# Issuing the copies of the block means from GpSimd's queue in place of SyncE's, in an attention and expert kernel

## The chip, the cores and the metric

The kernel runs on one core of a Trainium2 chip. The metric is the device time of one execution, in microseconds (us). Several executions are timed and the median is taken; one more execution is recorded by the hardware profiler, and all rows shown here come from that one. The engines are TensorE (PE in the rows, with PEld for its weight loads), VectorE (DVE), ScalarE (ACT), GpSimd (POOL) and SyncE (SP). The last two also issue DMAs; SPq and POOLq are their queues of such instructions.

## The reference

The program chains three layers in float32. The change lies in the first one, the attention, which is cut down here to what it computes; the two that follow are a mixture of 8 experts (each of 1536 tokens goes to two of them) and a dense layer with squared ReLU.

```python
def _attn_ref(q, k, v):                       # (2, 8, 768, 64) each
    B, H, S, D = q.shape
    block, window = (32, 16)
    nb = S // block                           # 24 blocks
    k_sum = k.reshape(B, H, nb, block, D).max(axis=3)
    v_sum = v.reshape(B, H, nb, block, D).mean(axis=3)
    scores_l = scale * q @ k^T, kept where |i - j| < window
    scores_s = scale * q @ k_sum^T + log(block)
    a = softmax(concat([scores_l, scores_s]))
    return a @ concat([v, v_sum])

x = moe(attention output)                     # top 2 of 8 experts, w1, relu, w2
return moe2(x)                                # w_in, relu squared, w_out
```

Each query thus sees its near keys and, for every block of 32 positions, one key (the maximum of the block) and one value (the mean of the block).

## The kernel before

**Units and tiles.** The 2 x 8 heads are worked in pairs: a unit u (0 to 7) is a batch and a pair of heads (u = 4 b + hp). For each unit SyncE loads three tiles from DRAM: `kB` (keys of both heads, 2 DMAs of 200 KB), `qt` (queries, 384 KB) and `vB` (values, 576 KB). `vB` holds 12 windows of 96 positions, so that 96 partitions by 12 x 128 elements come from DRAM; partitions 96 to 119 of every window take the 24 block means of the unit. There are LBUF = 4 buffers of each kind, so unit u + 4 takes the buffers of unit u once that one is done with.

**The block means.** `vmean(u)` (line 303) lets TensorE work out the 24 means from the loaded part of `vB`, 12 matmuls into one PSUM tile; `vcopy(u)` (line 317) is VectorE's copy of that to the tile `vm`, of which there are two buffers; `vstore(u)` (line 321) copies `vm` into the last 24 partitions of `vB`, the same 6 rows into all 12 windows, by four DMAs of 36 KB each. For unit 0 two engine copies (`vput`, lines 311 and 313) do this instead, so seven units have a `vstore`, 28 DMAs in all.

**The rest of the attention.** A step s is a unit and one or two tiles of 128 queries. `scores` (line 336, TensorE), `least` (line 347, VectorE: mask and row minimum), `expo` (line 354, ScalarE), `trans` (line 362, TensorE), `e_copy` (line 366, ScalarE), `pv` (line 377, TensorE: needs the whole of `vB`, the means included) and `x_cols` (lines 385 and 387). Then, by tiles g of 128 tokens (0 to 11; 6 of each batch), `rows` (line 397) and `x_row` (line 401) turn the result into rows; `gate_cols`, `gate_copy`, `gate_turn` and `gate_rows` (lines 432 to 451) compute the gates; `route` (lines 455 to 578; its matmuls are lines 500 to 511, its slots lines 518 and 522) finds each token's slot at its two experts; `scatter` (line 421) lets GpSimd write the rows to their slots in the DRAM buffer `xg` by indirect DMAs, two of them per tile. When the 18 scatters of tiles 0 to 8 have landed, SyncE loads the first expert's tokens (`x_load(0)`, line 213); tiles 9 to 11 reach that expert by one-hot matmuls (line 470). With that done, the experts' matmuls begin (lines 748 to 750), and they fill TensorE to the end of the program.

**What sets the order.** All of the attention is put in order by `Plan`, a list scheduler that runs while the kernel is written out. A `node` has an engine letter (P TensorE, V VectorE, A ScalarE, G GpSimd, D SyncE's queue), a cost in us, the nodes it depends on, and a `wait` that is added to its end for those who depend on it (for a load, LW = 0.9). The scheduler picks the node that can start first, with the longest remaining chain ahead among these, and writes out its instructions; each engine then runs its instructions in that fixed order. So a node's engine, cost and wait move the instructions of other engines too. A buffer is free for its next user when the nodes named by `plan.free` are over: the reload of `vB` for unit u + 4 is released by the last `pv` of unit u.

```python
    def load(cost, fn, *deps, **kw):
        return node("D", cost, fn, *deps, wait=LW, **kw)
    ...
    pn = node("P", 0.33 * n, lambda s=s: pv(s), cn, *vst[u], take=("v",))
    ...
    plan.free(v0, "w", vm, *pv_u[u])
```

SyncE's queue runs in order, and its loads are chained (`seq`, `after`) as kB, qt, vB of unit 0, then of unit 1, and so on. A DMA on SyncE's queue also waits until the one eight places ahead of it on that queue has landed.

Of the kernel before, what the change touches and what calls it, by code (L numbers as in the profile page):

```python
# [28 lines left out]
NQB = S // QB  # L29
WK = QB + 2 * WIN  # L30
# [19 lines left out]
LBUF = 4  # L50
# [25 lines left out]
class Plan:  # L76
# [6 lines left out]
    def node(self, eng, cost, fn, *deps, take=(), wait=0.0, after=()):  # L83
        n = {"id": len(self.nodes), "eng": eng, "cost": cost, "fn": fn, "deps": deps, "after": after, "take": take,
             "wait": wait, "free": {}}
        self.nodes.append(n)
        return n
# [48 lines left out]
def moe_pipeline_kernel(ctx: ExitStack, tc: tile.TileContext, qT, kT, vW, mk, idm, wg, noise, w1, w2, out):  # L136
    nc = tc.nc
# [97 lines left out]
    def attention(ctx):  # L235
# [15 lines left out]
        vB = [ac.tile([128, NQB, 128], F32, name=f"vB{i}") for i in range(LBUF)]  # L251
# [18 lines left out]
        node = plan.node  # L270
# [22 lines left out]
        p_t, e_t, et_t, xrow, z_t = {}, {}, {}, {}, {}  # L293
# [13 lines left out]
        def vput(a, eng):  # L307
            h = NQB // 2
            o, i = vB[0][WK:NS, a * h:a * h + h, :], p_t["m", 0][WK:NS, None, 0:128].to_broadcast([NB, h, 128])
            if a:  # L310
                nc.scalar.activation(out=o, in_=i, func=AF.Copy)
            else:
                v.tensor_copy(out=o, in_=i)

        def vcopy(u):
            p_t["c", u] = wk.tile([128, 128], F32, name="vm", bufs=2)
            v.tensor_copy(out=p_t["c", u], in_=p_t["m", u][:, 0:128])

        def vstore(u):
            for c in range(4):  # L320
                nc.sync.dma_start(out=vB[u % LBUF][WK + 6 * c:WK + 6 * c + 6],
                                  in_=p_t["c", u][32 * c:32 * c + 6, None, :].to_broadcast([6, NQB, 128]))

        def cols(b, hp, t):
            return xT[b][hp][:, t * 128:(t + 1) * 128]
# [263 lines left out]
        def load(cost, fn, *deps, **kw):  # L589
            return node("D", cost, fn, *deps, wait=LW, **kw)  # L590

        km, sc, ld_v, vst, qn, prev = {}, {}, {}, {}, {}, []
# [3 lines left out]
        for u in range(len(heads)):  # L596
# [25 lines left out]
            vm = node("P", 0.75 if u else 2.6, lambda u=u: vmean(u), ld_v[u], id_n, take=("v",))  # L622
            if u:
                vc = node("V", 0.2, lambda u=u: vcopy(u), vm, take=("vm",))
                vst[u] = [load(0.41, lambda u=u: vstore(u), vc)]
                plan.free(vm, "v", vc)
                plan.free(vc, "vm", *vst[u])
            else:
                vst[u] = [node("V", 0.85, lambda: vput(0, None), vm), node("A", 0.7, lambda: vput(1, None), vm)]
                plan.free(vm, "v", *vst[u])  # L630
            if u == 1:
# [3 lines left out]
                    out=xg[0:CAP, :].rearrange("r d -> (r d)").rearrange("(p a c) -> p a c", p=128, a=4),  # L635
                    in_=zt[:, None, :].to_broadcast([128, 4, CAP])), set_n, after=[wvals_n])
# [5 lines left out]
        for s, (b, hp, t0, n) in enumerate(order):  # L642
            u = b * HP + hp
# [92 lines left out]
    with ExitStack() as actx:  # L736
        attention(actx)
# [634 lines left out]
```

## Time and profile before

| | us |
|---|---|
| median of 3 runs (lowest, highest) | 696.1 (695.59, 696.43) |
| the profiled execution: its time | 692.52 |
| the profiled execution: its span | 690.5 |
| TensorE busy over the span | 640.0 (93%) |
| VectorE busy | 440.9 (64%) |
| ScalarE busy | 365.7 (53%) |
| GpSimd busy | 100.0 (14%) |

The span is the time from the first instruction to the last in the profile, and the time of that execution is 2.0 us more. The profiled execution is 3.6 us shorter than the median of the runs. Issuing a DMA is not counted as busy time on SyncE. In a row of a timeline stand the start in us from the span's start, the length in us, the engine, the line of the kernel, the operation, the tile that it writes and those that it reads, and the number of instructions merged into the row; in square brackets the idle time of the engine ahead of it, and what ended that. Most of TensorE's float32 matmuls stand twice in the trace: 8 instructions of `pv` are 16 records.

### The profile page before, as it was taken

The numbers are of one execution on the slowest core, as the hardware profiler recorded it, in microseconds if no ns is written. First come the engines' busy times: TensorE is split into PE (matmuls) and PEld (weight loads), VectorE is DVE, ScalarE is ACT, GpSimd is POOL, SyncE is SP. The second block draws the span as 40 slices with busy tenths as digits, with TensorE's granted clock in tenths as the row PEclk, the third lists the DMA queues.
The fourth block names the chain that finished last, engine by engine and source line by source line (L and its number), as shares of the span: only waits on it lengthen the run. The fifth ranks groups of instructions, "written<-read, shape, count | busy, mean of one in ns | idle before, by whom it ended". The sixth has DMA issues, their size and how long they took to land. (4 is left out here: it accounts for less than half of the span.)

```text
span 690.5 us, 11121 instructions
## 1 busy us (share of the span) xinstructions
PE 640.0 (93%) x3928; PEld 572.5 (83%) x3928; DVE 440.9 (64%) x980; ACT 365.7 (53%) x708; POOL 100.0 (14%) x171
## 2 busy tenths in 40 slices
PE   5697866799999999999999999999999999999995
PEld 4576646698999999999999998888878888788884
DVE  5567744686778887767777867666554566554442
ACT  3594551256566656666667666655443544433431
POOL 3000244420101000610004000310042100200002
PEclk9999977799999999999999999999999999999998
DMA  8969435478999998889889898665446544342201
GB/s 205 198 165 211 130 123 166 160 255 288 311 322 289 332 260 292 211 272 265 257 222 391 246 309 244 241 185 159 144 127 207 158 150 122 108 136 91 93 1 64
DMA packets 75740, 139.98 MB, mean 203 GB/s; under 512 B 9041, under 2 KB 44161, under 8 KB 74894
## 3 DMA queue, kind: packets, MB, share of 16 engines
q1 hardware_dynamic: 69566, 116.95, 58.0%
q0 software_dynamic: 6112, 22.25, 8.6%
q8 instruction: 33, 0.54, 0.3%
q14 instruction: 29, 0.24, 0.1%
HBM read 103.27 MB, written 34.88 MB: 200 GB/s over the span
## 5 line engine op out<-in xcount | busy, mean ns | idle before, releaser
L748 PE MATMUL ph<-xh,wh 128*128 128x512 f32 (+8 forms) x448 | 162.8, 363 | 1.8 <-ACT xh L1188 1.8
L750 PE MATMUL ph<-xl,wh 128*128 128x512 f32 (+8 forms) x448 | 162.7, 363 | 1.5 <-DVE xl L1189 1.2
L749 PE MATMUL ph<-xh,wl 128*128 128x512 f32 (+8 forms) x448 | 162.4, 363 | 0.0
L192 DVE TENSOR_TENSOR wl<-wr,wh 128x1024 fp32r<-128x1024 f32 x112 | 136.8, 1221 | 35.2 <-ACT wh L188 32.2
L188 ACT ACTIVATE wh<-wr 128x1024 fp32r<-128x1024 f32 x112 | 117.6, 1050 | 10.3 <-DMA wr<-in_w_dram 7.1
L750 PEld LDWEIGHTS ph<-xl,wh 128*128 128x128 f32 x448 | 84.2, 188 | 10.4 <-DVE xl L1189 2.1
L748 PEld LDWEIGHTS ph<-xh,wh 128*128 128x128 f32 x448 | 84.3, 188 | 10.1 <-ACT xh L1188 2.6
L749 PEld LDWEIGHTS ph<-xh,wl 128*128 128x128 f32 x448 | 84.3, 188 | 7.4
L750 PE MATMUL acc<-hl,wh 128*128 128x416 f32 (+7 forms) x256 | 87.8, 343 | 1.3 <-DVE hl L772 1.3
L749 PE MATMUL acc<-hh,wl 128*128 128x416 f32 (+7 forms) x256 | 87.7, 342 | 0.0
L748 PE MATMUL acc<-hh,wh 128*128 128x416 f32 (+7 forms) x256 | 87.7, 342 | 0.0
L765 ACT ACTIVATE hr<-ph 128x512 f32<-128x512 f32 x48 | 28.7, 598 | 100.3 <-PE ph L750 97.8
L766 DVE SCALAR_TENSOR_TENSOR hg<-ph,hr 128x512 f32<-128x512 f32 x48 | 33.2, 692 | 70.1 <-ACT hr L765 68.2
L749 PE MATMUL acc<-wh,hl 128*128 128x512 f32 x192 | 74.8, 390 | 0.0
L750 PE MATMUL acc<-wl,hh 128*128 128x512 f32 x192 | 74.7, 389 | 0.0
L748 PE MATMUL acc<-wh,hh 128*128 128x512 f32 x192 | 74.7, 389 | 0.0
L771 ACT ACTIVATE hh<-ph 128x416 fp32r<-128x416 f32 (+7 forms) x64 | 32.1, 502 | 80.2 <-PE ph L750 74.8
L772 DVE SCALAR_TENSOR_TENSOR hl<-ph,hh 128x416 fp32r<-128x416 f32 (+7 forms) x64 | 36.5, 570 | 34.5 <-ACT hh L771 32.0
L769 DVE TENSOR_TENSOR hl<-hg,hh 128x512 fp32r<-128x512 f32 x48 | 33.3, 694 | 33.5 <-ACT hh L768 32.8
L768 ACT ACTIVATE hh<-hg 128x512 fp32r<-128x512 f32 x48 | 30.3, 632 | 38.9 <-DVE hg L766 38.0
L354 ACT ACTIVATE es<-z,bi 128x120 f32<-128x120 f32 x96 | 36.6, 383 | 25.9 <-DVE bi L347 25.9
L750 PEld LDWEIGHTS acc<-hl,wh 128*128 128x128 f32 x256 | 48.2, 188 | 1.8 <-DVE hl L772 1.7
(246 smaller groups left out, 915.5 us busy)
## 6 DMA issues: line engine op xcount, KB each, us to landing
wr<-in_w_dram SPq DMA_DIRECT2D x64, 512.0 KB
wr<-w2f SPq DMA_DIRECT2D x48, 512.0 KB
cr<-in_w_dram SPq DMA_DIRECT2D x32, 512.0 KB
w2f<-c SPq DMA_DIRECT2D x32, 256.0 KB
vB<-in_vW_dram SPq DMA_DIRECT2D x8, 576.0 KB
xin<-xg SPq DMA_DIRECT2D x20, 208.0 KB
kB<-in_kT_dram SPq DMA_DIRECT2D x16, 200.0 KB
yg<-ys SPq DMA_DIRECT2D x16, 192.0 KB
```

The source lines that it names most:

```text
L188: nc.scalar.activation(out=hi_t[i], in_=raw_t[i], func=AF.Copy)
L192: nc.vector.tensor_tensor(out=lo_t[i], in0=raw_t.pop(i), in1=hi_t[i].bitcast(F32), op=OP.subtract)
L354: nc.scalar.activation(out=e_t[s][:, i, h], in_=z, func=AF.Exp, bias=bi, scale=-1.0, accum_out=sums[:, b * QT + t0 + i, c:c + 1])
L748: nc.tensor.matmul(out=o, lhsT=wh, rhs=xh, start=first, stop=False)
L749: nc.tensor.matmul(out=o, lhsT=wl, rhs=xh, start=False, stop=False)
L750: nc.tensor.matmul(out=o, lhsT=wh, rhs=xl, start=False, stop=last)
L765: nc.scalar.activation(out=r[:, 0:n], in_=p[:, 0:n], func=AF.Relu)
L766: nc.vector.scalar_tensor_tensor(out=gg[:, 0:n], in0=p[:, 0:n], scalar=0.0, in1=r[:, 0:n], op0=OP.max, op1=OP.mult)
L768: nc.scalar.activation(out=hh[:, 0:n], in_=gg[:, 0:n], func=AF.Copy)
L769: nc.vector.tensor_tensor(out=hl[:, 0:n], in0=gg[:, 0:n], in1=hh[:, 0:n].bitcast(F32), op=OP.subtract)
L771: nc.scalar.activation(out=hh[:, 0:n], in_=p[:, 0:n], func=AF.Relu)
L772: nc.vector.scalar_tensor_tensor(out=hl[:, 0:n], in0=p[:, 0:n], scalar=0.0, in1=hh[:, 0:n].bitcast(F32), op0=OP.max, op1=OP.subtract)
```

## The change

The four DMAs of `vstore` are issued on GpSimd's queue, and in the plan the node moves from SyncE's queue (cost 0.41, wait 0.9) to GpSimd (cost 2.5, wait 2.0).

```diff
         def vstore(u):
             for c in range(4):
-                nc.sync.dma_start(out=vB[u % LBUF][WK + 6 * c:WK + 6 * c + 6],
-                                  in_=p_t["c", u][32 * c:32 * c + 6, None, :].to_broadcast([6, NQB, 128]))
+                nc.gpsimd.dma_start(out=vB[u % LBUF][WK + 6 * c:WK + 6 * c + 6],
+                                    in_=p_t["c", u][32 * c:32 * c + 6, None, :].to_broadcast([6, NQB, 128]))
 
         def cols(b, hp, t):
             return xT[b][hp][:, t * 128:(t + 1) * 128]
@@ -622,7 +622,7 @@
             vm = node("P", 0.75 if u else 2.6, lambda u=u: vmean(u), ld_v[u], id_n, take=("v",))
             if u:
                 vc = node("V", 0.2, lambda u=u: vcopy(u), vm, take=("vm",))
-                vst[u] = [load(0.41, lambda u=u: vstore(u), vc)]
+                vst[u] = [node("G", 2.5, lambda u=u: vstore(u), vc, wait=2.0)]
                 plan.free(vm, "v", vc)
                 plan.free(vc, "vm", *vst[u])
```

The two lines move instructions on every engine of the attention. Three places follow. In the names, `vB0_112` is the buffer of `vB` for units 0 and 4, `vB1_113` for 1 and 5, `vB2_114` for 2 and 6, `vB3_115` for 3 and 7; `kB_116` to `kB_119` are the same for the keys; `L303` is `vmean`, `L377` is `pv`.

SyncE's queue, from the load of unit 7's values on, as a piece of the difference (minus: before, plus: the change):

```order
 L603 DMA qt<-in_qT_dram 128x768
 L606 DMA vB_115<-in_vW_dram 96x1536
-L321 DMA vB_112<-vm 6x12x128 x4
-L321 DMA vB_113<-vm 6x12x128 x4
-L182 DMA wr<-in_w_dram 128x1024
-L321 DMA vB_114<-vm 6x12x128 x4
-L182 DMA wr<-in_w_dram 128x1024
-L321 DMA vB_115<-vm 6x12x128 x4
-L182 DMA wr<-in_w_dram 128x1024
+L182 DMA wr<-in_w_dram 128x1024 x3
 L213 DMA xin<-xg 32x13x128 x4
```

The copies of units 4 to 7 leave the queue behind the last load, and those of units 1 to 3 leave it between the loads of unit 4; on GpSimd all 28 stand ahead of the first scatter.

TensorE, from the first `pv` of unit 3 to the last `pv` of units 1, 2 and 3, before:

```order
L377 MATMUL pv_747<-et_725,vB3_115 64x64 x8
L362 MATMUL pt_764<-idz_78,es_547 120x128 x4
L362 MATMUL pt_771<-idz_78,es_606 120x128 x4
L432 MATMUL pv_780<-xh_128,wg_sb_121 32x384 x2
L432 MATMUL pv_780<-xl_129,wg_sb_121 32x384 x2
L362 MATMUL pt_788<-idz_78,es_652 120x128 x4
L377 MATMUL pv_796<-et_778,vB1_113 64x64 x8
L377 MATMUL pv_807<-et_786,vB2_114 64x64 x8
L377 MATMUL pv_818<-et_805,vB3_115 64x64 x8
```

and the same place in the change:

```order
L377 MATMUL pv_743<-et_722,vB3_115 64x64 x8
L362 MATMUL pt_760<-idz_78,es_550 120x128 x4
L362 MATMUL pt_770<-idz_78,es_606 120x128 x4
L303 MATMUL pv_778<-vB0_112,idz_78 32x128 x12
L362 MATMUL pt_796<-idz_78,es_664 120x128 x4
L432 MATMUL pv_804<-xh_128,wg_sb_121 32x384 x2
L432 MATMUL pv_804<-xl_129,wg_sb_121 32x384 x2
L377 MATMUL pv_815<-et_792,vB1_113 64x64 x8
L377 MATMUL pv_826<-et_794,vB2_114 64x64 x8
L377 MATMUL pv_837<-et_813,vB3_115 64x64 x8
```

`vmean(4)`, which reads the newly loaded `vB0_112`, now stands ahead of the last `pv` of units 1, 2 and 3, which release the reloads of `vB1_113`, `vB2_114` and `vB3_115`.

TensorE around the first matmul of the routing of tiles 0 to 5 (`L500`), before:

```order
L362 MATMUL pt_1234<-idz_78,es_1108 120x128 x2
L377 MATMUL pv_1239<-et_1223,vB3_115 64x64 x8
L377 MATMUL pv_1253<-et_1232,vB3_115 64x64 x4
L377 MATMUL pv_1261<-et_1249,vB2_114 64x64 x4
L500 LDWEIGHTS ones_81
L500 MATMUL pv_1266<-rowb_82,ones_81 128x48
L336 MATMUL ps_1268<-kB2_118,qt_853 64x2x96 x2
```

and in the change, from the last of the count matmuls of that routing (`L511`) on:

```order
L511 MATMUL pv_1240<-mall_85,ones_81 128x8
L336 MATMUL ps_1270<-kB0_116,qt_445 64x2x96 x2
L336 MATMUL ps_1270<-kB0_116,qt_445 64x2x24 x2
L377 MATMUL pv_1281<-et_1221,vB3_115 64x64 x8
L377 MATMUL pv_1302<-et_1238,vB3_115 64x64 x4
L377 MATMUL pv_1311<-et_1249,vB2_114 64x64 x4
```

The `pv` of unit 7 (`vB3_115`) stood ahead of the routing of tiles 0 to 5, and now stands behind all of its matmuls. On GpSimd, the ninth scatter, where it was the eleventh, is the first one of a row (`xrow`) that is made behind the first matmul of the second routing (tiles 6 to 8): four tiles are scattered ahead of it instead of five, and five instead of four from it to the end of tile 8. Between `vmean(6)` and `vmean(7)` TensorE also does 20 matmuls of `pv` of units 4 and 5 more than before, and one group of 4 in `trans` and one `rows` less.

## Rows read from the trace of the kernel before

**Rows 1.** Two stretches: busy us of PE, PEld, DVE, ACT, POOL, then PEclk, DMA share, GB/s.

```profile
0.00:137.00 137.00, 98.83 (x1226) 80.20 (x1227) 80.32 (x374) 63.16 (x251) 32.22 (x65) 0.86 0.64 171
137.00:500.00 363.00, 361.38 (x1918) 345.27 (x1917) 266.63 (x493) 225.79 (x349) 44.09 (x75) 1.00 0.84 261
```

**Rows 2.** The same, two stretches of the attention.

```profile
44.00:62.00 18.00, 12.51 (x234) 9.63 (x234) 10.15 (x34) 9.44 (x35) 0.00 (x0) 0.99 0.98 226
...
82.00:97.00 15.00, 9.14 (x91) 6.34 (x90) 5.42 (x32) 5.63 (x26) 10.75 (x20) 0.84 0.45 176
```

**Rows 3.** Timeline of SyncE's queue, 43 to 76 us.

```profile
43.98 0.35 SPq L606 DMA_DIRECT2D vB<-in_vW_dram  x1
44.38 1.19 SPq L599 DMA_DIRECT2D kB<-in_kT_dram  x2
...
49.40 0.34 SPq L606 DMA_DIRECT2D vB<-in_vW_dram  x1
...
58.43 8.55 SPq L321 DMA_DIRECT2D vB<-vm  x8
...
72.11 3.08 SPq L321 DMA_DIRECT2D vB<-vm  x4
```

**Rows 4.** Timeline of TensorE, 47 to 82 us.

```profile
47.31 0.52 PE L432 MATMUL pv<-xh,wg_sb 128*32 128x384 f32 x2
...
48.09 0.65 PE L362 MATMUL pt<-idz,es 128*120 128x128 f32 x4
48.67 1.62 PE L377 MATMUL pv<-et,vB 120*64 120x64 f32 x48
...
61.41 1.41 PE L303 MATMUL pv<-vB,idz 96*32 96x128 f32 x24 [1.80 <-DMA vB<-in_vW_dram]
...
67.63 0.86 PE L303 MATMUL pv<-vB,idz 96*32 96x128 f32 x24
...
70.28 1.35 PE L377 MATMUL pv<-et,vB 120*64 120x64 f32 x40
...
78.03 1.50 PE L377 MATMUL pv<-et,vB 120*64 120x64 f32 x32 [2.87 <-DMA vB<-vm]
...
81.09 1.10 PE L336 MATMUL ps<-kB,qt 128*64 128x192 f32 x8
```

**Rows 5.** Timeline of VectorE: the maxima of unit 5, a copy to vm, the first slots.

```profile
50.10 2.00 DVE L291 TENSOR_REDUCE kB<-kB 64x24 f32<-64x768 f32 x2 [3.27 <-DMA kB<-in_kT_dram]
...
69.38 0.29 DVE L317 COPY vm<-pv 128x128 f32<-128x128 f32 x1
...
81.20 0.26 DVE L518 TENSOR_TENSOR sl<-pv,mall 128x96 f32<-128x96 f32 x1 [0.63 <-PE pv L511]
```

**Rows 6.** One line's instructions, lengths in ns as shortest/median/longest: vstore, scatter, a later fill.

```profile
L321 SPq DMA_DIRECT2D vB<-vm x28: 720/726/1376, 24.5 to 74.5; - x28
...
L421 POOL DMA_INDIRECT xg<-xrow,slot_i x24: 968/972/1154, 82.1 to 134.3; - x24
...
L857 POOL DMA_INDIRECT xg<-z,tb_gi x7: 937/938/1856, 151.8 to 228.8; - x7
```

**Rows 7.** Timeline of GpSimd: first and last scatter of two bursts.

```profile
82.11 1.15 POOL L421 DMA_INDIRECT xg<-xrow,slot_i  x1 [74.56 <-DVE bi L347]
...
93.77 0.97 POOL L421 DMA_INDIRECT xg<-xrow,slot_i  x1 [0.22 <-issue]
...
104.68 0.97 POOL L421 DMA_INDIRECT xg<-xrow,slot_i  x1 [9.85 <-DVE sl L518]
...
113.61 0.97 POOL L421 DMA_INDIRECT xg<-xrow,slot_i  x1 [0.23 <-issue]
```

**Rows 8.** Timeline of TensorE and VectorE in the second burst.

```profile
110.35 0.29 PE L377 MATMUL pv<-et,vB 120*64 120x64 f32 x3 [1.07 <-issue]
...
114.63 0.42 DVE L385 COPY xh<-pv 128x256 f32<-128x256 f32 x1 [5.63 <-remote]
```

**Rows 9.** VectorE's first use of the first expert's loaded tokens.

```profile
130.89 2.08 DVE L219 STREAM_TRANSPOSE xtt<-xin 128x416 f32<-128x416 f32 x4
```

## The prediction

> **What bounds the kernel now.** I read the stretches first. From 137 us on TensorE is busy without a break (361 of 363 us), while in the first 137 us it works 98.8 [rows 1]. The experts can't start before the attention ends, and nothing behind them waits for SyncE or GpSimd, so what the change is worth is the shift of that point, us for us. The queues come next. SyncE issues the copies of the block means from 24.5 to 75 us [rows 6]; those of units 4 to 7 stand behind all loads, eight of them taking 8.55 us and the last four 3.08 [rows 3]. In this middle part the DMA engines are 98% busy from 44 to 62 us [rows 2], and TensorE waits for a load at 61.41 and for the copies of unit 7 at 78.03, 2.87 us long [rows 4]. From 82 us on GpSimd issues the scatters in bursts of ten and eight [rows 7]; in these TensorE has gaps of 1.1 us that no wait of the profile explains, and VectorE, idle for 5.63 us, goes on at 114.63 [rows 8], just as the last scatter of the burst is issued (113.61 + 0.97 = 114.58). TensorE is busy in 9.1 of the 15 us from 82 to 97 us [rows 2].
>
> **The change, part by part.** SyncE loses 28 DMAs of 0.73 us, GpSimd gets them. The ones of units 1 to 3 end nothing: no row of TensorE waits for them now, and GpSimd is idle between its set-up and 82.11 us [rows 7]; I count them at nothing. If they came late, `pv` of units 1 to 3 would stall, each by what the copy takes longer. The weight loads behind them on SyncE's queue come earlier, but feed the experts, behind the attention: nothing. What counts is the four places where the order moves.
>
> *The values of unit 4.* `vmean(4)` now stands at the place that TensorE reaches at 47.31 us [rows 4]. Its load is issued at 43.98 [rows 3], when the last `pv` of unit 0 is over, and that place has not moved. It lands shortly before the keys of unit 5, which are queued behind it and are used from 50.10 us on [rows 5]: half of these are 200 KB, 0.9 us at 226 GB/s [rows 2], so it lands near 49.2. TensorE stalls by 1.9 us (bounds: nothing, if it lands by 47.31; 2.8, if only at 50.10). Behind the stall, in order, are `vmean(4)` (0.86, as the row at 67.63), a group of `trans` (0.65), the gate matmuls (48.09 - 47.31 = 0.78) and the last `pv` of unit 1 (a third of 1.62) [rows 4]: 49.2 + 0.86 + 0.65 + 0.78 + 0.54 = 52.0. That `pv` releases the next load of values, issued at 49.40 now [rows 3]: 2.6 us later, and the loads of units 6 and 7 stand behind it. What is queued until then (576 + 400 + 384 KB, 6.0 us at 226 GB/s from some 2 us after 43.98) is through at 52, so the DMA engines run dry for about that long. I take 2.0 us for the loads of units 6 and 7, between 0 and 2.6.
>
> *The copies of unit 7.* `vmean(6)` goes from 61.41 to 63.4. From there to `vmean(7)` are 6.2 us now; TensorE gets 20 more `pv` matmuls there (1.35, the row at 70.28) and loses a `trans` group (0.65) [rows 4], so `vmean(7)` starts at 70.3, against 67.63. VectorE's copy starts 1.75 us after it (69.38) and takes 0.29 [rows 5], so GpSimd can begin at 72.3. How long a plain DMA takes GpSimd to issue no row shows. The nearest are its own scatters, 0.97 us with 0.22 between [rows 6, 7]; SyncE's 0.73 for this very copy is the low bound, the longest fill, 1.86, the high one [rows 6]. With 1.19 four end at 77.1 (bounds 75.2 and 80.6). Now the last issue ends at 75.19 and TensorE goes on at 78.03 [rows 3, 4], 2.8 us later; so they land at 79.9 (78.0 to 83.4).
>
> *The routing of tiles 0 to 5 ahead of `pv` of unit 7.* From the end of `vmean(7)` (68.49) to the first slots are 12.7 us now [rows 4, 5]. Out of these fall the wait (2.87), the `pv` of unit 7 and of the last tile of unit 6 (1.50) and the 1.35 done before: 7.0 remain, so slots come at 78.2 instead of 81.20, 3.0 us earlier. `pv` of unit 7 then waits for 79.9, and ends 1.5 us later, at 81.4. The same work is done now at 82.1, when TensorE is through with the group of scores whose row begins at 81.09 [rows 4] and ends at 82.19, its last matmul overlapping the next by some 0.1. So TensorE is 0.7 us ahead. The late loads have eaten most of the 2.87.
>
> *The scatters.* The first burst starts 3.0 us earlier, at 79.1, with eight in place of ten. At their spacing of 1.3 us [rows 7] it ends near 89.4, where it now ends at 94.7. The second holds ten in place of eight, and lasts 2.6 us longer. The load of the first expert's tokens can only follow it, but is used at 130.89 [rows 9], 16.3 us behind the burst's end now; that covers the 2.6. But VectorE and TensorE were held up to the end of this burst [rows 8], so the 2.6 are on the path. The first burst gives back at most 5.3 us; I take 4.0, since 5.9 of the 15 us from 82 to 97 are idle on TensorE [rows 2] and a part of them is VectorE's and ScalarE's chain. Bounds: 0 and 5.3.
>
> **The sum:** 0.7 + 4.0 - 2.6 = 2.1 us earlier. The profiled execution would go from 692.5 to 690.4. The median of the runs stands 3.6 above that execution, so I forecast 696.1 - 2.1 = **694.0**. With every bound at its good end (no late load 2.0, the whole 5.3) it is 5.4 us earlier; at the bad end (load 0.6 later, copies 3.5 later, nothing back) 6.0 us later, 702.
>
> **Rivals.**
>
> *The longer second burst decides (slower).* Place: GpSimd, from 104.7 us on. If the gaps in the first burst are not on the path, because ScalarE's chain would have filled that time, what is left is -0.7 + 2.6 = +1.9: 698.0. It decides as soon as the first burst gives back less than 1.9 us. For it: VectorE resumes exactly at that burst's end [rows 8]. Against it: the first burst shows the same kind of gaps. Chance 0.20.
>
> *GpSimd's issue is held up by VectorE (slower).* The 24 scatters took 0.97 to 1.15 us [rows 6] in a stretch where VectorE is busy 80 of 137 us [rows 1], which speaks against it; one fill of seven took 1.86. If the copies of unit 7 all took that, they would land at 83.4, and `pv` would stall 3.5 us more: -2.1 + 3.5 = +1.4, 697.5. Chance 0.10. The Trainium skill, "SBUF — State Buffer", section "SBUF: two separate sides", says that GpSimd can't write its DMA descriptors while VectorE runs an operation that takes both ports, and advises to issue from SP instead. By that rule this rival is what happens; the scatters' narrow spread does not bear it out here.
>
> *Nothing to tell (no change).* The first burst gives back 2 us instead of 4: -0.1, 696.0. For it: the middle part is bound by loads, the DMA engines 98% busy [rows 2], and SyncE's queue is not what they wait for. Chance 0.22. The Trainium skill, "DMA: Bandwidth & Descriptors", section "Issuing engines are not separate DMA queues", holds that DMAs from any engine share the same 16 DMA engines, and that spreading them saves only the time of issuing; by it alone this rival would be the likeliest. No row here has such a copy on GpSimd, so none shows it.
>
> That the change doesn't do what it says is no rival: the order shows all 28 copies on GpSimd.
>
> **How the numbers follow.** A measurement of this kernel can tell some 0.2% (1.4 us) from no change. Forecast (faster): 0.48, its own range 691.0 to 694.7. No change: 0.22. Slower: 0.20 + 0.10 = 0.30, around 698. The range leaves out the far end of the bounds on both sides, under 1 in 10 each: 691.0 to 699.5.
>
> **What would show it.** TensorE should stall near 47 us for `vB`, and the load of unit 5's values be issued near 52 instead of 49.40. The copies on GpSimd should take about 1 us each, and the last wait for `vB<-vm` be about 1 us, not 2.87. The first scatter should start near 79, the first burst have eight, the second ten. The experts' first matmul should start some 2 us earlier than before. I am wrong if the copies take over 1.5 us, if TensorE shows unexplained gaps during the new copies too, or if it is held up in the first burst as long as before.

## The result, and the profile after

The changed kernel takes 703.39 us (median of 4 runs, 701.25 to 707.85) against 696.26 for the kernel before beside it (695.59 to 697.77): a ratio of 1.011, interval 1.0071 to 1.0149. A second, longer series gave 1.0103 (1.0070 to 1.0135). The forecast was 694.0 with a range up to 699.5; the change makes the kernel 1% slower. The profiled execution took 701.25 us, with a span of 699.2 (before: 692.52 and 690.5).

GpSimd's timeline of the changed kernel, the copies of units 4 to 7 (one row each) and the first and last scatter of the two bursts:

```profile
50.95 2.30 POOL L321 DMA_DIRECT2D vB<-vm  x4 [15.48 <-ACT et L366]
62.25 2.30 POOL L321 DMA_DIRECT2D vB<-vm  x4 [9.00 <-DVE vm L317]
67.35 2.30 POOL L321 DMA_DIRECT2D vB<-vm  x4 [2.80 <-DVE vm L317]
79.84 2.30 POOL L321 DMA_DIRECT2D vB<-vm  x4 [10.19 <-DVE u L557]
...
86.74 1.07 POOL L421 DMA_INDIRECT xg<-xrow,slot_i  x1 [4.52 <-DVE bi L347]
...
96.92 0.97 POOL L421 DMA_INDIRECT xg<-xrow,slot_i  x1 [0.23 <-issue]
...
104.50 0.97 POOL L421 DMA_INDIRECT xg<-xrow,slot_i  x1 [6.53 <-DVE sl L518]
...
116.00 0.97 POOL L421 DMA_INDIRECT xg<-xrow,slot_i  x1 [0.22 <-issue]
```

GpSimd issues a copy in 0.58 us (2.30 for four), faster than SyncE's 0.73 [rows 6]. The first burst starts at 86.74, where 79.1 was forecast and 82.11 was the time before [rows 7]; it has eight scatters and ends at 97.89. The second starts at 104.50, as before (104.68), has ten, and ends at 116.97 in place of 114.58.

TensorE's timeline, the three values' means and the waits around them (they answer to [rows 4]):

```profile
48.66 0.86 PE L303 MATMUL pv<-vB,idz 96*32 96x128 f32 x24 [1.96 <-DMA vB<-in_vW_dram]
...
58.58 1.51 PE L303 MATMUL pv<-vB,idz 96*32 96x128 f32 x24 [3.86 <-DMA vB<-in_vW_dram]
...
65.23 0.86 PE L303 MATMUL pv<-vB,idz 96*32 96x128 f32 x24
...
75.50 1.12 PE L377 MATMUL pv<-et,vB 120*64 120x64 f32 x16 [6.45 <-DMA vB<-vm]
78.23 0.89 PE L303 MATMUL pv<-vB,idz 96*32 96x128 f32 x24
```

`vmean(4)` waits 1.96 us, as forecast (1.9), and the load of unit 5's values goes out at 51.55 (forecast 52.0). Then two things stand here that the forecast has not: `vmean(5)` waits 3.86 us for those late values, and `pv` of unit 5 waits 6.45 us for its own copies, which GpSimd had begun to issue at 62.25. `vmean(7)` starts at 78.23, not at 70.3. `pv` of unit 7 waits for nothing:

```profile
86.20 1.12 PE L377 MATMUL pv<-et,vB 120*64 120x64 f32 x32
```

Stretches of the changed kernel (start:end and length, then busy us of PE, PEld, DVE, ACT, POOL, granted clock, DMA share, GB/s), and the last of them in the kernel before:

```profile
62.00:82.00 20.00, 13.51 (x181) 11.15 (x180) 10.76 (x61) 8.85 (x40) 6.77 (x12) 0.76 0.78 163
82.00:97.00 15.00, 13.05 (x192) 9.67 (x190) 11.86 (x68) 10.12 (x37) 8.94 (x17) 1.00 0.33 114
...
160.00:180.00 20.00, 15.79 (x73) 15.16 (x72) 9.98 (x23) 9.78 (x17) 0.94 (x1) 0.83 0.82 261
```

```profile
160.00:180.00 20.00, 18.38 (x97) 17.54 (x96) 15.87 (x35) 12.48 (x20) 2.06 (x2) 1.00 1.04 309
```

From 82 to 97 us TensorE is idle for 1.95 us where it was 5.86 [rows 2]. These 3.9 us are near the 4.0 of the forecast, but not all of them are the burst's: in the changed kernel the scatters begin only at 86.74. Over the first burst itself TensorE is idle for 4.7 of 12.6 us before and for 2.6 of 11.2 us now, so the burst gives back 2.2 us, and they had been spent already, in the wait of 6.45. SyncE's queue shows what else was released, the three weight loads from 59.52 on, which stood at 67.02, 71.55 and 75.23 before:

```profile
51.55 0.33 SPq L606 DMA_DIRECT2D vB<-in_vW_dram  x1
...
59.52 3.39 SPq L182 DMA_DIRECT2D wr<-in_w_dram  x3
118.73 1.91 SPq L213 DMA_DIRECT2D xin<-xg  x4
```

The experts' first matmul starts at 140.21 (136.67 before), and behind it another 5 us are lost: 559.0 us to the end of the span against 553.8.

### The profile page after: what moved, and what is told of

It is laid out like the page before. It is cut to its first block, busy times and chain, and to the rows that moved or that the text cites. A ratio compares the mean times of both kernels' runs of the same rounds, so it can differ in the third digit from the quotient of the medians.

```text
span 699.2 us, 11134 instructions
## 1 busy us (share of the span) xinstructions
PE 644.7 (92%) x3928; PEld 576.4 (82%) x3928; DVE 440.4 (63%) x980; ACT 365.7 (52%) x708; POOL 116.8 (17%) x199
## 3 DMA queue, kind: packets, MB, share of 16 engines
q1 hardware_dynamic: 67382, 115.92, 56.5%
## 5 line engine op out<-in xcount | busy, mean ns | idle before, releaser
L748 PEld LDWEIGHTS acc<-hh,wh 128*128 128x128 f32 x256 | 48.6, 190 | 1.0 <-ACT hh L771 0.9
```

The costliest lines, as they stand in the source:

```text
L748: nc.tensor.matmul(out=o, lhsT=wh, rhs=xh, start=first, stop=False)
```

## The experiments

All ratios are to the kernel before, timed in the same series; the series ran on different chips. The table gives, for every trace, the first scatter, the start of the second burst and the end of its last scatter, the experts' first matmul and the rest (span less that start), all in us.

| run | ratio (interval) | first scatter | second burst | experts | rest |
|---|---|---|---|---|---|
| before | | 82.11 | 104.68 to 114.58 | 136.67 | 553.8 |
| r1, before again | | 83.58 | 106.96 to 116.84 | 141.88 | 556.0 |
| r2, before, third | | 83.08 | 106.45 to 116.33 | 141.37 | 558.6 |
| after | 1.011 (1.0071, 1.0149) | 86.74 | 104.50 to 116.97 | 140.21 | 559.0 |
| r3, after again | | 90.51 | 106.94 to 119.38 | 142.20 | 558.5 |
| r4, after, timed | 1.0103 (1.0070, 1.0135) | 89.11 | 106.88 to 119.30 | 142.92 | 558.3 |
| e1, order, copies on SyncE | 1.0051 (1.0017, 1.0086) | 89.36 | 106.73 to 120.11 | 141.73 | 559.9 |
| r8, order, copies behind loads | 1.0062 (1.0028, 1.0096) | 88.16 | 105.71 to 118.14 | 143.45 | 553.8 |
| e2, queue | 1.0066 (1.0028, 1.0104) | 88.07 | 109.78 to 119.64 | 144.68 | 558.9 |
| e3, after, weights held | 1.0104 (1.0058, 1.0150) | 83.06 | 105.29 to 117.73 | 141.44 | 557.4 |
| e4, queue, weights held | 1.0105 (1.0048, 1.0162) | 85.31 | 109.07 to 118.95 | 141.19 | 558.9 |
| r5, after, ten and eight | 1.0096 (1.0060, 1.0132) | 88.98 | 109.13 to 119.02 | 140.93 | 562.2 |
| r6, copies on ScalarE | 1.0267 (1.0186, 1.0348) | 103.86 | 124.79 to 137.23 | 160.27 | 555.8 |
| r7, before, twelve and six | 1.0035 (1.0003, 1.0067) | 85.99 | 108.65 to 115.98 | 136.92 | 556.2 |
| r9, after, early zero rows | 1.0037 (1.0007, 1.0067) | 87.39 | 105.00 to 117.46 | 141.54 | 554.7 |
| r10, before, early zero rows | 0.9966 (0.9935, 0.9996) | 82.53 | 106.41 to 116.30 | 139.05 | 554.3 |
| r14, the same again | 0.9991 (0.9961, 1.0021) | 85.22 | 108.58 to 118.46 | 142.97 | 555.2 |

### The two halves of the change, and the weight loads

e1 undoes the queue and keeps the order; e2 keeps the order of before and changes the queue; e3 and e4 add a transfer of 4 bytes ahead of the weight loads, which needs the last `vm`.

```diff
 e1 (against the change)
-                nc.gpsimd.dma_start(out=vB[u % LBUF][WK + 6 * c:WK + 6 * c + 6],
+                nc.sync.dma_start(out=vB[u % LBUF][WK + 6 * c:WK + 6 * c + 6],
 e2 (against the kernel before)
-                nc.sync.dma_start(out=vB[u % LBUF][WK + 6 * c:WK + 6 * c + 6],
+                nc.gpsimd.dma_start(out=vB[u % LBUF][WK + 6 * c:WK + 6 * c + 6],
 e3 (against the change), e4 (against e2)
...
+        wl, w_held = [], lambda: (nc.sync.dma_start(out=mark, in_=p_t["c", 7][0:1, 0:1]), w_load())
+        for i in range(RBUF):
+            wl.append(load(1.45, w_load if i else w_held, *([] if i else [vc]), after=[last, *wl[-1:]]))
```

> The changed kernel's order on every compute engine, with the 28 copies issued by SyncE again, in SyncE's own queue ahead of the weight loads. If the copies on GpSimd cost the time (theory A: TensorE's wait of 6.45 us at 75.50 is for copies that land late), this wait is under 1.5 us here and the time is near the kernel before, 693 to 697 us. If the new order costs it (theory B: the early mean of unit 4, its late loads, ten scatters in the second burst), the time stays at 700 us or more, whoever issues the copies.

> The order of the kernel before on TensorE, VectorE and ScalarE, with the copies issued by GpSimd; the three weight loads then stand directly behind the last value load on SyncE's queue. Theory A: a wait of 4 us or more for the copies of some unit from 5 to 7 appears, and the time is 699 to 704 us. Theory B: no such wait, 694 to 697 us.

> The changed kernel, but the first weight load waits on SyncE's queue for VectorE's last copy of means (near 79 us), by a transfer of 4 bytes ahead of it; every other engine's order is that of the changed kernel. Theory A1 (the weight loads, freed from behind the copies, crowd the DMA engines from 60 us on and delay GpSimd's copies): TensorE's wait of 6.45 us falls under 2 us, the first scatter comes 3 us or more earlier than 86.74, the time is 695 to 699 us. Theory A2 (copies issued by GpSimd land some 10 us late under any load of the hardware queues, the value and key loads of units 6 and 7 being enough): the wait stays over 4 us and the time at 700 to 704 us.

> The order of the kernel before, copies on GpSimd, weight loads held until VectorE's last copy of means. Theory A1: no wait of more than 2 us for copies, and a time of 694 to 697 us, under that of the kernel without the hold. Theory A2: the same waits and the same time, within 1 us, as without the hold. Theory B: as the kernel before, 694 to 697 us, with or without the hold.

Each half alone costs about half a per cent (1.0051 and 1.0066), so neither theory A nor theory B is the whole. e1 was less clean than meant: copies of units 4 and 5 stood ahead of loads on SyncE's queue, and TensorE waited 5.75 us for `vB`:

```profile
64.23 1.50 PE L303 MATMUL pv<-vB,idz 96*32 96x128 f32 x24 [5.75 <-DMA vB<-in_vW_dram]
```

In e2 TensorE's longest wait for copies is 1.79 us, where theory A expected 4 or more. But the late copies cost time there on VectorE. There are two buffers of `vm`, so `vcopy(6)` has to wait until unit 4's copies have landed, and `vcopy(7)` until unit 5's have:

```profile
72.69 0.29 DVE L317 COPY vm<-pv 128x128 f32<-128x128 f32 x1 [2.85 <-DMA vB<-vm]
...
77.55 0.29 DVE L317 COPY vm<-pv 128x128 f32<-128x128 f32 x1 [3.05 <-DMA vB<-vm]
```

In the kernel before VectorE waits 0.44 us there, once, at 67.53. The hold did to the wait what theory A1 said in part, and to the time nothing. TensorE's waits for the copies in e3:

```profile
70.97 1.12 PE L377 MATMUL pv<-et,vB 120*64 120x64 f32 x16 [3.70 <-DMA vB<-vm]
...
85.54 1.73 PE L377 MATMUL pv<-et,vB 120*64 120x64 f32 x32 [2.86 <-DMA vB<-vm]
```

The wait for unit 5 falls from 6.45 to 3.70, the first scatter comes 3.7 us earlier, but the weight loads (76.39) now meet the copies of unit 7, and the second burst starts at 105.29. From the semaphores of the DMAs in the traces, the end of a group's issue and the time from there to its last landing:

```text
copies of            issued until   landed   later by
after, unit 4            53.25       60.09      6.8
after, unit 5            64.55       75.37     10.8
after, unit 6            69.65       78.44      8.8
after, unit 7            82.14       85.03      2.9
e3 (hold), unit 5        63.02       70.84      7.8
e3 (hold), unit 6        67.95       71.64      3.7
e3 (hold), unit 7        78.17       85.41      7.2   weight loads issued at 76.39
e2, unit 4               63.18       72.56      9.4
e2, unit 5               65.47       77.43     12.0
before, unit 4 (SyncE)   62.02       67.41      5.4
before, unit 7 (SyncE)   75.19       77.90      2.7
```

A copy that GpSimd issues thus lands some 3 us after its issue in a quiet stretch, 7 to 8 beside the value and key loads or the weight loads, and 9 to 12 with both. SyncE's copies of the kernel before land 2.2 to 5.4 us after theirs; unit 4's, right behind the last loads, are the latest. So the late landing of theory A is there. That the time follows from it is not shown: e3 shortens TensorE's wait for unit 5 from 6.45 to 3.70 us and e4 VectorE's wait for the `vm` buffers from 5.9 to 2.5 us, and neither kernel is faster for it.

### How far the traces repeat

> The kernel before, unchanged, profiled once more. The five other traces so far have 557 to 560 us from the experts' first matmul to the end and a wait of VectorE for the second expert's tokens that ends 29.5 to 30.3 us behind that matmul; the trace of before has 553.8 and 27.3. If this is a property of the kernel before (its queues leave the fill of the tokens alone), this trace has 553 to 555 and 27 to 28 again, at any total time. If the one trace of before was a lucky execution, this one shows 556 us or more and 29 us or more, and then those 5 us are not the change's.

> The same kernel a third time, with the same question; beside it, how far the start of the experts' first matmul (136.67 us in the first trace) moves from one execution of one kernel to another: under 1 us if the five traces' 140.2 to 144.7 are to be read as shifts by the changes.

> The changed kernel, unchanged, profiled once more: the wait for the copies of unit 5 (6.45 us at 75.50), the first scatter (86.74) and the experts' first matmul (140.21) should return within 1 us if they belong to the kernel and not to one execution.

The trace of before on which the prediction rests was at the short end: of the 29 runs of the kernel before in the series of r4, one is under its 692.52 us (691.10). The experts start at 136.67, 141.88 and 141.37 us in three executions of one kernel, so single shifts of 3 us there can't be read as the change's. In r3 the first scatter came 3.8 us and the experts 2.0 us later than in the first trace of the change, where I had expected them within 1 us. What returns in all three traces of the changed kernel is the wait for unit 5 (6.45, 6.68 and 6.07 us; 4.96 in r9, whose attention is the same) and the late first scatter. The second burst starts when it did before and ends 2.6 us later on average (118.55 against 115.92). With r9 on the one side and r10 and r14 on the other, whose attention is also unchanged, it ends 1.8 us later, where traces of one kernel differ by up to 3.9 us; the first scatter comes 5.1 us later.

### The burst

r5 has ten scatters in the first burst and eight in the second again, with the copies on GpSimd; r7 has twelve and six in the kernel before.

```diff
-            s0 = node("V", 0.06 + 0.02 * n, slots, b1)
+            s0 = node("V", 0.06 + 0.02 * n, slots, b1, after=[xr_n[g] for g in range(5)] if g0 == 0 else [])
```

(r7 has 6 in place of 5, in the kernel before.)

> The changed kernel, unchanged, timed in the same series as the three others. From the first series: 1.011 of the kernel before, 0.7 to 1.5% slower. In its trace the wait for the copies of unit 5 (6.45 and 6.68 us in two traces) again between 6 and 7 us.

> The changed kernel, with the rows of tile 4 turned ahead of the first slots, so that ten scatters can go in the first burst and eight are left for the second, as in the kernel before; all 28 copies stay on GpSimd. If the longer second burst decides (the prediction's first rival), the second burst ends 2.5 us earlier against the first burst's end, the experts start some 2.5 us earlier than in the changed kernel, and the time is 2 to 3 us under it, 0.6 to 0.8% over the kernel before. If the late copies decide, the wait of 6 to 7 us for unit 5 stays, what the second burst gains the first loses, and the time is within 1 us of the changed kernel.

> The kernel before (copies on SyncE), with the rows of tiles 3 to 5 turned ahead of the first slots, so that twelve scatters can go in the first burst and six are left for the second. If the length of the second burst is on the path, the experts start 2 to 2.6 us earlier than in the kernel before (136.7, 141.9 and 141.4 us in three traces) and the time is 0.997 of it. If the first burst, longer by 2.6 us, takes as much away from TensorE as the second gives, the ratio is 0.999 to 1.002.

The split of the scatters moves nothing. In r5 the second burst ends at 119.02, since it starts at 109.13, 2.2 us after that of r4: what the shorter second burst saves, the longer first one costs. In r7 it ends as early as before (115.98) and the time is 1.0035. So the first rival had the right row (the second burst ends later) and the wrong lever: it is not the number of scatters in a burst. What it is instead these runs don't show.

### The order without GpSimd, cleaner, and the copies on a third engine

r6 lets ScalarE issue the copies, at the places where the plan had put them for GpSimd (`nc.scalar.dma_start` in place of `nc.gpsimd.dma_start`). r8 has the order of the change with SyncE's copies, those of units 4 to 6 behind all loads:

```diff
         def vstore(u, held=[]):
+            held += [u] * (u < 8)
+            while held and (u < 4 or "v7" in p_t):
...
 (in load_v)
-                nc.sync.dma_start(out=vB[u % LBUF][0:WK], in_=vW[heads[u]])
+                nc.sync.dma_start(out=vB[u % LBUF][0:WK], in_=vW[heads[u]]); u == 7 and (p_t.update(v7=1), vstore(8))
```

> The order of the changed kernel on TensorE, VectorE and SyncE, unchanged; ScalarE issues the 28 copies on its own hardware queue, at the places where the plan put them. If the late landing of GpSimd's copies is the cause, the copies of unit 5 land within 4 us of their last issue, TensorE's wait for them is under 2 us, the first scatter comes near 80 us, as the prediction had it, and the time is 4 us or more under the changed kernel (1.000 to 1.004 of the kernel before). If the new order is the cause, the time stays at 1.008 or more. If ScalarE's 28 issues (0.6 to 0.8 us each by SyncE's rows) hold up its exponentials, TensorE waits for ScalarE instead, some 2 us at each of units 4 to 7.

> The changed kernel's order on TensorE (to the last instruction); SyncE issues the copies again, those of units 1 to 3 where the plan puts them, those of units 4 to 6 behind the last value load and ahead of the weight loads, as in the kernel before. If the late landing of GpSimd's copies is the cause in the attention, TensorE's wait of 6 to 7 us for unit 5 is gone (under 1.5 us), the first scatter comes at 78 to 83 us in place of 86.7 to 90.5, and the time is 1.000 to 1.004 of the kernel before. If the new order costs the time by itself (unit 4's early mean, the later loads, ten scatters in the second burst), the first scatter may come early, but the experts start at 140 us or later and the ratio is 1.007 or more.

r6 is the slowest of all. ScalarE's timeline and TensorE's:

```profile
82.67 5.28 ACTq L321 DMA_DIRECT2D vB<-vm  x4
88.00 0.87 ACT L366 ACTIVATE et<-pt 120x512 f32<-120x512 f32 x2 [5.26 <-DMA vB<-vm]
```

```profile
88.93 1.55 PE L377 MATMUL pv<-et,vB 120*64 120x64 f32 x24 [3.57 <-ACT et L366]
```

Four issues hold ScalarE for 5.28 us and TensorE waits behind it: a copy's issue has to go to an engine that nothing waits for. r8 has the order without GpSimd. SyncE's queue and TensorE's waits in it (the copies are line 322 there):

```profile
56.20 0.33 SPq L606 DMA_DIRECT2D vB<-in_vW_dram  x1
...
62.91 15.15 SPq L322 DMA_DIRECT2D vB<-vm  x12
```

```profile
61.79 1.18 PE L303 MATMUL pv<-vB,idz 96*32 96x128 f32 x24 [2.42 <-DMA vB<-in_vW_dram]
...
74.75 1.12 PE L377 MATMUL pv<-et,vB 120*64 120x64 f32 x16 [3.98 <-DMA vB<-vm]
...
76.85 1.55 PE L377 MATMUL pv<-et,vB 120*64 120x64 f32 x24
...
79.67 0.86 PE L303 MATMUL pv<-vB,idz 96*32 96x128 f32 x24
```

With no copy on GpSimd the wait for unit 5's copies is gone: they land at 76.67, and unit 5's `pv` (the last 16 of the 24 records at 76.85) waits for nothing. But 3.98 us are now lost on unit 4's copies, which the change itself does not wait for. r8 issues them only from 62.91 on, behind the last load, and they land at 74.62. The first scatter still comes at 88.16, and the ratio is 1.0062. So the order loses time with SyncE's queue too, each time at another place: in r8 copies come late behind the loads, in e1 a load comes late behind copies (5.75 us). Neither run tells which part of the 6.45 us is GpSimd's.

### Behind the attention: a fill that meets VectorE

Two transfers of GpSimd write zeros to rows of the experts' token buffer that hold no token: one of 24 rows for all experts (line 930), and the fill of the second expert's rows (line 857), which waits until the first has landed. Only then does SyncE load the second expert's tokens. Two executions of the kernel before, first r1, then r2: VectorE's split of a weight tile, the fill, and the load.

```profile
157.57 1.23 DVE L192 TENSOR_TENSOR wl<-wr,wh 128x1024 fp32r<-128x1024 f32 x1 [0.35 <-ACT wh L188]
...
156.87 0.94 POOL L857 DMA_INDIRECT xg<-z,tb_gi  x1 [3.93 <-DVE tb_pre L944]
...
162.33 1.93 SPq L213 DMA_DIRECT2D xin<-xg  x4
```

```profile
157.06 1.23 DVE L192 TENSOR_TENSOR wl<-wr,wh 128x1024 fp32r<-128x1024 f32 x1 [0.35 <-ACT wh L188]
...
157.43 1.67 POOL L857 DMA_INDIRECT xg<-z,tb_gi  x1 [5.00 <-DVE hl L772]
...
164.11 1.93 SPq L213 DMA_DIRECT2D xin<-xg  x4
```

In r1 the fill starts 0.70 us ahead of the split and takes 0.94 us; in r2 it starts inside the split, takes 1.67 and ends 0.81 us behind the split's end. Against the experts' first matmul the load goes out 20.45 us later in r1, 22.74 in r2, and the rest lasts 556.0 and 558.6 us. The changed kernel:

```profile
155.90 1.23 DVE L192 TENSOR_TENSOR wl<-wr,wh 128x1024 fp32r<-128x1024 f32 x1 [0.35 <-ACT wh L188]
...
155.95 2.00 POOL L857 DMA_INDIRECT xg<-z,tb_gi  x1 [4.67 <-DVE hl L772]
...
163.41 1.95 SPq L213 DMA_DIRECT2D xin<-xg  x4
```

The fill starts 0.05 us into the split, takes 2.00, and ends 0.82 us behind it. In all nine traces in which the fill starts inside the split (0.05 to 0.87 us into it), its issue ends 0.81 to 0.82 us behind the split's end. Of the kernels with GpSimd's copies all seven traces lose this race (after, r3, r4, r5, e2, e3, e4); of the seven without, two (r2, e1). r9 and r10 take it away: the row numbers of the 24 rows are worked out first and their transfer is issued at once.

```diff
+        ri, gf = tbp.tile([128, 1], I32, name="tb_ri"), t("gf", E)
+        tt(ri[0:n3], p[0:n3, 1, 0:1], rc[0:n3], OP.add)
+        nc.gpsimd.indirect_dma_start(out=xg, out_offset=bass.IndirectOffsetOnAxis(ap=ri[0:n3, 0:1], axis=0),
+                                     in_=z4[0:n3, 0:DM], in_offset=None)
         v.tensor_copy(out=cnt, in_=p[:, 0, 0:E])
...
```

> The changed kernel, with the 24 zero rows of the experts' last groups sent off at once when their row numbers are there, 2.3 us earlier, so that GpSimd's fill of the second expert's tokens, which waits for them, starts before VectorE's split of the weights at 15.7 us behind the experts' first matmul. If the late fill is part of the loss, the second expert's tokens are loaded at 18 to 19 us behind that matmul in place of 22.9 to 23.2, the rest of the program lasts 553 to 556 us in place of 558 to 559, and the time is 3 to 5 us under the changed kernel (1.003 to 1.006 of the kernel before). If it is not, the tokens come earlier and the time stays at 1.010.

> The same edit in the kernel before, which lost the race in one of three traces. If the race is worth 2.6 us where it is lost (its two traces at 556.0 and 558.6 us behind the experts' first matmul), this kernel gains 1 to 3 us, the ratio is 0.995 to 0.998, and the gap to the changed kernel with the same edit is smaller than 1.0%. If nothing behind the attention is on the path, 1.000.

> The kernel of r10, unchanged, in a series of its own. If the race it takes away is real, the ratio is 0.994 to 0.999 again, and the second expert's tokens are loaded at 20.3 to 20.9 us behind the experts' first matmul. If the first ratio was the spread of the runs, 0.999 to 1.003.

The fill and the load in r9:

```profile
156.40 0.95 POOL L857 DMA_INDIRECT xg<-z,tb_gi  x1 [5.55 <-DVE tb_pre L944]
```

```profile
161.87 1.95 SPq L213 DMA_DIRECT2D xin<-xg  x4
```

The changed kernel goes from 1.0103 to 1.0037, in two series whose intervals don't overlap, and its rest from 558.6 (the mean of three) to 554.7. In the kernel before the same edit gave 0.9966 once and 0.9991 in a second series, so it is not shown to beat that kernel; no run here does. So the edit takes 0.66% off the changed kernel and 0.1 to 0.3% off the kernel before, and only the difference, 0.3 to 0.6 of the 1.0%, is what the race adds to the change's cost; each of these ratios has an interval of some 0.3% either way. With the edit in both, in one series, the changed kernel is still 4.5 us slower (700.10 and 695.57; without it 5.4 in the series of r4). The loads came at 20.3 us, not at the 18 to 19 that I expected: the 24 rows go out 1.75 us earlier (8.39 in place of 10.14 behind the first matmul), not 2.3, and the fill then waits for VectorE's `tb_pre`.

### The halves once more, without that race

> The kernel of r8 (the changed order, copies by SyncE behind the loads) with the early zero rows of r9 and r10. Compared with the kernel before with these rows (0.9966) and the changed kernel with them (1.0037). If GpSimd's late copies cost the 0.7%, this one is at 0.996 to 0.999. If the new order costs them, it is at 1.002 to 1.005. By the end of the second burst alone (118.1 us in the trace of r8, 116.3 in that of r10) it would be 1.8 us over r10, 0.999.

> The kernel of e2 (the order of the kernel before, copies by GpSimd) with the early zero rows. If GpSimd's late copies cost the 0.7%, it is at 1.002 to 1.005; if the new order, at 0.996 to 0.999. By the end of the second burst alone (119.6 us in the trace of e2 against 116.3) it would be 3.3 us over r10, 1.0013.

> The kernel of e3 (the changed kernel, weight loads held until VectorE's last copy of means) with the early zero rows. If the weight loads' crowding is in the loss, it is 2 us or more under the changed kernel with these rows, at 0.998 to 1.001. If not, within 1 us of it, 1.002 to 1.005. By the end of the second burst alone (117.7 us in the trace of e3, 117.5 in that of r9) it would be the same.

These ran on another chip, on which the kernel before takes 680.58 us (18 runs): the order alone 1.0105 (1.0058 to 1.0151), the queue alone 1.0039 (1.0008 to 1.0070), the whole change with the weights held 1.0088 (1.0053 to 1.0124). The intervals of order and queue overlap, so neither is shown to cost more. What the hold is worth there is open, since no run of the change without it stands beside. The figures can't be set beside 0.9966 and 1.0037, as I had meant to, since the chip differs in the very stretch in question (last section).

## Why the prediction was wrong, point by point

- *The values of unit 4.* Right in place and size: 1.96 us at 48.66, and the next load at 51.55. Its consequence was short: the late load of unit 5 costs `vmean(5)` 3.86 us at 58.58, where I took 2.0 for the later loads; `vmean(6)` starts at 65.23, not at 63.4.
- *The copies of unit 7.* The step that failed. I counted the 20 `pv` matmuls that move ahead of `vmean(7)` as 1.35 us of work, and let that mean start at 70.3. Twelve of them are unit 4's (`vB0_112`), whose copies had landed by then, and eight are unit 5's (`vB1_113`): they need unit 5's copies, which I had priced nowhere: "the four places" had only those of unit 7. In the trace they cost 6.45 us. With the 1.8 us by which `vmean(6)` is late they put `vmean(7)` at 78.23 and the first scatter at 86.74, 7.6 us behind the forecast. The late landing is a part of it: unit 5's copies land 10.8 us behind their issue, where I had 2.8 for unit 7's, from SyncE's in the kernel before. Some of the wait may go with the weight loads that I had written down as "nothing": with these held it is 3.70 us in e3, against 4.96 to 6.68 without. The issue itself I had too dear: 0.58 us, not 1.19, under my low bound of 0.73.
- *The routing ahead of `pv` of unit 7.* The distance was right: from `vmean(7)` to the first slots 7.6 us (78.23 to 85.83), where I had 7.9 (70.3 to 78.2). `pv` of unit 7 waits for nothing, where I had a last wait of about 1 us: its copies land at 85.03 and TensorE comes to it at 86.20.
- *The scatters.* The first burst gave back 2.2 us of TensorE's idle time, not 4.0, and what it gave only went to repay the wait ahead of it: the second burst starts at 104.50 to 106.94 in three traces of the change, at 104.68 to 106.96 in three of before. What is left of the sum is the loss of 2.6 us, without the gain of 4.0. By the end of the burst it is +2.6 (118.55 against 115.92), at the experts' start +1.8 (means of three traces each, 141.78 and 139.97). The latter rests on the first trace of before: the mean of its two others alone (141.88 and 141.37) is within 0.2 us of the change's.
- *The rivals.* The first, "the longer second burst decides", came nearest: its row is the one that the traces show, at +1.9 in the forecast and +1.8 to +2.6 measured. It was held at 0.20 and ended at 698, since nothing behind the attention was in it. Its lever, the number of scatters, was refuted by r5, so that the number came out is luck. The second, GpSimd held up by VectorE, does not happen at the copies (28 of them at 0.58 to 0.83 us), but it does at the fill, 70 us later, for +2.4: the mean rest of three traces each is 558.6 against 556.2, and r9 gives 0.66% back, of which the kernel before gains 0.1 to 0.3 too. The third, no change, is out: neither interval reaches below 1.007.
- *What I had bounded wrongly.* "Nothing behind them waits for SyncE or GpSimd" was read from TensorE's busy time; one load there hangs on GpSimd, with 0.7 us to spare in r1.
- *What stays open.* 1.8 and 2.4 us make 4.2; the medians differ by 5.4 and 7.1. One to three us have no row, and the 1.8 is not clear of the spread of the traces; which part of the 1% the late copies cost is not shown. Why the traces of kernels with GpSimd's copies lose the race each time is not shown either: in the changed kernel two loads of SyncE go out 0.4 us later against the first matmul than in the kernel before (3.8 in place of 3.4 us), but r2 and e1 lose it at 3.4. And why the second burst does not start earlier when the first does (e3) was not settled.

The Trainium skill, "SBUF — State Buffer", section "SBUF: two separate sides", from which I had taken the second rival, says that a DMA issued by GpSimd stands still while VectorE holds the port that both share. The fill agrees: its issue ends 0.81 to 0.82 us behind the end of VectorE's split in both rows above, r2's and the change's, whenever it began. The Trainium skill's rule on issuing engines, "DMA: Bandwidth & Descriptors", section "Issuing engines are not separate DMA queues", by which only issue time is saved, falls short here: the landing changed too, 6.8 to 10.8 us behind GpSimd's issue for units 4 to 6, where SyncE's copies of these units in the kernel before land 2.2 to 5.4 us behind theirs.

## What to carry to other kernels

Where a step is moved to another queue, price the landing of every transfer of it, not of the last one alone, and ask of each consumer that the new order pulls forward whether its own input can be there by then, and of each buffer that the transfer frees who waits for it. A list scheduler that takes 2.0 us for a transfer that needs 7 to 12 under load will place its readers too early. And one trace of before is one execution: profile the unchanged kernel twice before you read shifts of a few us as a change's.

## What the hardware did that I had not expected

The gaps of TensorE in the bursts, on which the term of 4.0 us rested, belong to some executions only. On the chip of r11 and r12 TensorE works right through the scatters. The stretch 82:104, first r2 (before), then r11:

```profile
82.00:104.00 22.00, 15.95 (x151) 11.68 (x148) 10.30 (x73) 9.72 (x48) 10.74 (x20) 0.73 0.31 120
```

```profile
82.00:104.00 22.00, 21.24 (x332) 18.18 (x330) 21.29 (x127) 18.62 (x75) 13.50 (x24) 1.00 0.45 165
```

TensorE is busy for 21.24 us in place of 15.95. The orders of these two differ; pairs with the same order in this stretch are r8 and r11 (19.29 and 21.24 us) and e2 and r12 (14.93 and 21.35). In r11 all 18 scatters follow each other up to 111.70, and the experts start at 126.55 us, 10 to 16 us earlier than in the traces of the kernel before and the changed one. r13, on the same chip, has the two bursts and a start at 131.41. No run here tells what the gaps hang on.

The granted clock adds to the spread: in the stretch from 128 to 136 us, behind TensorE's sparse work in the second burst, it was 0.88 in the first trace of before and 0.50 (1.2 GHz) in r1:

```profile
128.00:136.00 8.00, 6.74 (x31) 4.81 (x30) 3.94 (x11) 0.52 (x1) 4.15 (x7) 0.88 0.28 108
```

```profile
128.00:136.00 8.00, 6.40 (x22) 5.30 (x23) 5.43 (x23) 0.00 (x0) 3.00 (x6) 0.50 0.23 87
```

The same four matmuls of line 470 (`ps<-xtt,idz`) took 1.56 us in the one and 2.98 in the other. From the first matmul of that line to the experts' start it was 10.62 us in the one (126.05 to 136.67) and 13.54 in the other (128.34 to 141.88), so 2.9 of the 5.2 us between the two arise there.
